# A gated mix of two attentions: VectorE's exps of attention B as a cubic, for scores bounded by a check

## The chip, the cores and the metric

The kernel runs on one core of one Trainium2 chip. The metric is the device time of one execution in microseconds (us). A "tile" below is one block of softmax numerators, 128 partitions by 1024 elements.

## The reference

Two attentions read the same input x (2048 tokens, 512 features) and are mixed by a gate per token:

```python
g = sigmoid((x * gate_w).sum(-1, keepdims=True))
a = A(x)   # 32 heads of 16 for q, one shared head for k and v; wq and wk are 8 times larger
b = B(x)   # 32 heads of 16 for q, k and v
out = g * a + (1 - g) * b
```

Each attention is softmax(q k^T / 4) v per head, followed by an output projection `wo`. All inputs are float32 draws of spread 0.05 (A's wq and wk then times 8). B's scores are therefore small, and A's are not.

## The kernel before

The scores of all heads are 2 x 32 x 2048 x 2048 numbers, which is 2048 tiles. No maximum is subtracted: an exp is taken of each score, the values are multiplied by it, and a column of ones beside the values gives the sum to divide by. That is safe only while scores are bounded, so the kernel collects absolute maxima of its inputs and intermediates in `stats` (`absmax`, L217), and near the end `flag_check` (L1058) turns them into a flag. When a bound is not met, `_general` runs after the fast path and computes all again.

**The work.** There are eight groups, alternating A and B, with eight heads each. A group has four phases (four of the heads, half of the queries), and a phase has 32 quads, which go over the keys. A quad is two tiles, with two heads each: their scores (a `score` call each, L630), their exps, and the products with the values (`values`, L682), summed over the phase in one PSUM pair of banks. At the end of a phase the sum is copied out (L747), normalised (`normalised`, reciprocals at L572), and the output products (`o_unit`, L496) add it into the output in DRAM. Products of the weights with x (`project`, L422) make q of both attentions and k and v of B for the phases to come; they are cut in steps of eight matmuls.

**Who takes the exps.** ScalarE takes nearly all (L641), from two PSUM tiles `sc` in turn. VectorE takes the rest: `vector_job` (L799) puts the scores of a tile into the spare PSUM pair `pair[1]`, and `chain` (L827) computes its exp in seven operations: a conversion from PSUM to a fixed-point power of two (L843), two integer passes that take out the mantissa and the exponent (L847, L851), and four multiply-adds (L856). Six tiles `vec` hold what VectorE works on. The spare pair is also where `project`, `o_unit` and the turning of v put their products, one at a time, until VectorE has emptied it.

**What sets the order.** The order of every instruction is fixed when the program is built, by a planner (`_Plan`, L80, and the loop of `pe_step`, L940) that keeps a clock for each engine and puts the next piece of work on TensorE or VectorE. ScalarE's scores come first. Between them TensorE takes, in this order, the values of VectorE's own quads, then the spare pair's work (`spare_job`, L900), then the values of ScalarE's quads. For the spare pair a tile of VectorE goes ahead of other products unless `hurry` (L891) finds one that would miss its due time. A tile of VectorE is begun only while

- at most 1500 ns of chain operations are queued on VectorE (`chained`, L796; 8500 for the second tile of a quad),
- at most three tiles are held by quads whose values aren't yet summed,
- the current phase has over 24,000 ns of ScalarE's exps left, beyond what is queued on VectorE; else a quad of the next phase is taken, if its q and k are there (`pick`, L768; in the last phase there is none).

On VectorE an operation has a rank (0 and 1: emptying a PSUM pair; 3: the chain; 3.2 to 3.5: normalising; 4: maxima), and the plan counts 1130 ns for a pass over a tile and 620 ns for an integer pass.

At the end the last group's output products are added to the output in SBUF (L515): `preload` (L1128) fetches it from DRAM once no other product is left, and the plan lets them begin 30 us later.

Of the kernel before, what the change touches and what calls it, by code (L numbers as in the profile page):

```python
# [20 lines left out]
P = 128  # L21
# [12 lines left out]
IN_MIN, IN_MAX = 2.0 ** -8, 16.0  # L34
QK_MAX = 4.0
S_MAX = 40.0


VEC = (0.14718679, 0.3602188, 0.76941108, -0.03925424)
LEAD = struct.unpack("I", struct.pack("f", 3.46474126))[0] & 0x7FFFFF  # L40
RANGED = ["v_a", "x", "gate", "wk_a", "wv_a", "wq_a", "wo_a", "wq_b", "wk_b", "wv_b", "wo_b", "v_b"]
KINDS = RANGED + ["q_a", "q_b", "k_a", "k_b"]
# [125 lines left out]
def _fast(ctx, tc, x, wq_a, wk_a, wv_a, wo_a, wqkv_b, wo_b, gate_w, out, flag):  # L168
# [33 lines left out]
    def rows(i):  # L202
        return slice(ROWS * i, ROWS * (i + 1))
# [218 lines left out]
    def project(part, src, gi, half, kind, can, due):  # L422

        state = {}
        need = ("w" + part, src, gi)
        name = f"{part}{src}{gi}{half}"

        def job(n):
            product(weights[src, gi, part], half, n, pair[1])

        def put(hilo, t):
            to = q_tiles(src, gi, half) if part == "q" else k_tiles(gi, half)
            parts = (0, 1, 0, 1) if part == "q" else (0, 0, 1, 1)
            for p in range(4):
                fns = lay(hilo, to[p], p, parts, (nc.sync, nc.gpsimd))
                done = max(plan.on_sp(fns[0::2], t, ISSUE_SP), plan.on_pool(fns[1::2], t, ISSUE))
                ready[part, src, gi, half, p] = done + LANDS
            free["hilo"] = done + LANDS - 4000

        def finish(t):  # L440
            hilo = []

            def hi():
                hilo.extend(halves_of(name))
                nc.vector.tensor_scalar(hilo[0], pair[1], UP ** -1, None, op0=ALU.mult)  # L445

            def lo():
                nc.vector.scalar_tensor_tensor(hilo[1], pair[1], UP ** -1, hilo[0], op0=ALU.mult, op1=ALU.subtract)

            def then(end):  # L450
                free["spare"] = end + FROM_VEC
                plan.vec(lambda: absmax(kind, 2 * gi + half, hilo[0], AX.XY), 1130, 4, end, due=end + 8000)
                if part == "v":
                    turned(gi, half, hilo, end)
                else:
                    put(hilo, end)

            free["hilo"] = math.inf
            one = plan.vec(hi, 1130, 1, t + TO_VEC)
            plan.vec(lo, 1130, 0, 0.0, (one,), then)  # L460

        return _Unit([(lambda n=n: job(n), PRODUCT) for n in range(len(STEPS))], finish,
                     lambda now: ready.get(need, math.inf) <= now and free["hilo"] <= now and can(), due, name, lambda now: can())

    def turned(gi, half, hilo, now):

# [293 lines left out]
        put_in[0] = 0  # L760


    def left_in(ph):

        lo = max(at[0], 32 * ph)
        return 2 * sum(1 for m in range(lo, 32 * ph + 32) if m not in vector) - (part[0] if lo == at[0] else 0)
# [60 lines left out]
    def chain(u, t):  # L827


        tiles = {}  # L830

        def tile(name):
            tiles[name] = free_vecs.popleft()
            return tiles[name]

        def give(*names):
            free_vecs.extend(tiles[name] for name in names)

        converts[0] += 1

        def convert():
            converts[0] -= 1
            nc.vector.tensor_scalar(tile("p").bitcast(I32), pair[1], SCALE / (UP * UP) / math.log(2) * 2.0 ** 23, None, op0=ALU.mult)  # L843

        def mantissa():
            tile("m"), tile("w")
            nc.vector.tensor_scalar(tiles["m"].bitcast(I32), tiles["p"].bitcast(I32), 0x7FFFFF, 125 << 23,  # L847
                                    op0=ALU.bitwise_and, op1=ALU.bitwise_or)

        def power():  # L850
            nc.vector.tensor_scalar(tiles["w"].bitcast(I32), tiles["p"].bitcast(I32), 0x7F800000, 0x40000000 | LEAD,  # L851
                                    op0=ALU.bitwise_and, op1=ALU.bitwise_xor)

        def horner(i):
            p, m, w = (tiles[k] for k in "pmw")
            nc.vector.scalar_tensor_tensor(p, m if i == 3 else p, VEC[i], m if i else w, op0=ALU.add, op1=ALU.mult)  # L856
            if i < 2:
                give("m" if i else "w")

        def spared(end):  # L860
            free["spare"] = end + FROM_VEC

        def over(end):
            probs[u] = tiles["p"]
            held[1] -= 1
            m = u // 2
            chains[m] = max(chains.get(m, 0), end)
            if all(x in probs for x in (2 * m, 2 * m + 1)):
                pending[quads[m][0]].append((m, end + FROM_VEC))

        def waits():
            return converts[0]

        def due(ns):
            return lambda: plan.act + left_in(quads[u // 2][0]) * EXP + (64 * EXP if quads[u // 2][0] > quads[min(at[0], len(quads) - 1)][0] else 0) - ns - 5000

        a = plan.vec(convert, 1130, 1, t + TO_VEC, (), spared, room=lambda: free_vecs)
        b = plan.vec(mantissa, 620, 3, 0.0, (a,), None, due(7000), lambda: len(free_vecs) >= 2 + waits())
        c = plan.vec(power, 620, 3, 0.0, (a, b), None, due(6300))
        d = plan.vec(lambda: horner(3), 1131, 3, 0.0, (b, c), None, due(5600))  # L880
        for i in (2, 1, 0):
            d = plan.vec(lambda i=i: horner(i), 1131, 3, 0.0, (d,), None if i else over, due(1300 * i + 1300))
# [175 lines left out]
    def flag_check():  # L1058
# [5 lines left out]
        nc.vector.tensor_scalar(lim[:, 2 * r : r + k], highest[:, r:k], QK_MAX, None, op0=ALU.is_lt)  # L1064
        nc.vector.tensor_mul(highest[:, ix("q_a") : ix("q_b") + 1], highest[:, ix("q_a") : ix("q_b") + 1],
                             highest[:, ix("k_a") : ix("k_b") + 1])
        nc.vector.tensor_scalar(lim[:, r + k : r + k + 2], highest[:, ix("q_a") : ix("q_b") + 1],
                                S_MAX / (DH * SCALE), None, op0=ALU.is_le)
        nc.vector.tensor_reduce(lim[:, 2 * k - 1 :], lim[:, 0 : r + k + 2], axis=AX.X, op=ALU.min)
        nc.vector.tensor_scalar(flag, lim[:, 2 * k - 1 :], -1.0, 1.0, op0=ALU.mult, op1=ALU.add)  # L1070

# [56 lines left out]
    def preload():  # L1128
        if "late" in ready or pv_at[0] < LASTS - 1 or current:
            return  # L1130
        if any(u for u in units) or any(op.rank == 1 for op in plan.ops) or wanted or loading:
            return
        for k in range(8):
            for e in range(2):
                t = 8 * (k // 4) + 4 * e + k % 4
                nc.sync.dma_start(late[:, k, e], out[t * P : (t + 1) * P, :])
        ready["late"] = plan.pe + 30000
# [65 lines left out]
    ready["ka", 0] = ready["va", 0] = 0.0  # L1203
    plan.vec(lambda: absmax("q_a", 0, hilo[0], AX.XY), 1130, 4, 8000.0, due=30000.0)
    plan.vec(k_top, 280, 4, 8000.0, due=30000.0)
    for k in range(5):
        plan.vec(lambda k=k: x_top(k), 1130, 4, 12000.0, due=50000.0)
    for k in range(4):
# [259 lines left out]
```

## Time and profile before

| | |
|---|---|
| runs, device time | 1824.4, 1826.82, 1826.92 us; median 1826.82 |
| span of the profiled execution, first to last instruction | 1822.2 us |
| granted TensorE clock, mean | 0.996 |
| TensorE matmuls | 1742.1 us busy (96%) |
| TensorE weight loads | 844.5 us busy (46%) |
| VectorE | 1332.0 us busy (73%) |
| ScalarE | 1778.7 us busy (98%) |
| exps on VectorE | 122 tiles |

The profile gives the profiled execution's span; its device time isn't given apart, and the three runs lie 2.2 to 4.7 us above that span. In the profile PE is TensorE, PEld its weight loads, DVE VectorE, ACT ScalarE, POOL GpSimd, and SP the queue of SyncE. A group of instructions has its source line, engine, operation, tiles and shape, its count, its busy time with the mean duration of one, and the idle time of its engine just before it with what ended that. Durations overlap: the next operation may start before the one ahead has ended. B's groups run from about 256 to 478, 701 to 919, 1141 to 1360 and 1583 us to the end.

### The profile page before, as it was taken

How to read it: one execution, taken by the hardware profiler on the slowest of the kernel's cores; microseconds unless marked ns; L12 is line 12 of the kernel's file. 1: busy time of each engine (PE TensorE's matmuls, PEld its weight loads, DVE VectorE, ACT ScalarE, POOL GpSimd, SP SyncE). 2: the span in 40 equal slices, each digit the busy share in tenths (PEclk: the TensorE clock that was granted, in tenths of full speed). 3: DMA queues.
4: the chain of work that ended last, by engine and by line, in shares of the span. 5: the costliest groups of instructions: out<-in, count | busy, mean ns of one | idle time of the engine just before them, and what ended most of it. 6: DMA issues, size and time to landing. Idle time of an engine off the chain costs nothing.

```text
span 1822.2 us, 95700 instructions
## 1 busy us (share of the span) xinstructions
PE 1742.1 (96%) x44697; PEld 844.5 (46%) x44697; DVE 1332.0 (73%) x1507; ACT 1778.7 (98%) x1942; POOL 305.1 (17%) x367
## 2 busy tenths in 40 slices
PE   8999999999999999999999999999999999999896
PEld 5544444444444444444444444444444444444442
DVE  5277656779667597869767569796967676788994
ACT  5999999999999999999999999999999999999995
POOL 2212001202020131231102023133200111012000
PEclk9999999999999999999999999999999999999998
DMA  5121111323121142433212123342312122236111
GB/s 152 36 61 44 46 58 55 90 55 67 32 62 32 39 83 55 75 65 66 44 42 63 32 66 56 67 84 63 64 20 57 44 55 57 42 67 149 36 61 61
DMA packets 64883, 109.39 MB, mean 60 GB/s; under 512 B 14480, under 2 KB 22928, under 8 KB 64480
## 3 DMA queue, kind: packets, MB, share of 16 engines
q0 software_dynamic: 21504, 43.99, 13.6%
q1 hardware_dynamic: 39744, 56.99, 11.4%
q8 instruction: 351, 5.75, 1.3%
q10 hardware_dynamic: 3232, 2.23, 0.4%
q14 instruction: 52, 0.43, 0.1%
HBM read 14.75 MB, written 33.55 MB: 27 GB/s over the span
## 4 chain that ended last, share of the span: by engine, by line
ACT 86%; issue 8%; PE 4%; DVE 1%; DMA 1%; ACTq 0%; POOL 0%; DVEq 0%
ACT prob L641 85%; PE pair L682 1%; PE sc L627 1%; PE pair L301 0%; DVE vec L856 0%; PE pair L1173 0%; DMA prob<-in_A_wv_dram 0%; DVE xT L1295 0%; DMA vec<-in_A_x_dram 0%; DVE xT L515 0%; DMA Qa<-loqa 0%; PE pair L335 0%; DVE dT L572 0%; ACT early L641 0%; PE pair L210 0%
## 5 line engine op out<-in xcount | busy, mean ns | idle before, releaser
L641 ACT ACTIVATE prob<-sc 128x1024 f32<-128x1024 f32 x1905 | 1749.7, 1134 | 3.8 <-PE sc L627 3.2
L682 PE MATMUL pair<-prob,vA 64*32 64x512 f32 (+1 forms) x8048 | 510.4, 566 | 0.0
L682 PE MATMUL pair<-prob,vB 64*32 64x512 f32 (+1 forms) x8016 | 508.4, 569 | 0.0
L856 DVE SCALAR_TENSOR_TENSOR vec<-vec,vec 128x1024 f32<-128x1024 f32 x366 | 445.9, 1242 | 2.8
L627 PE MATMUL sc<-Qb,K 64*32 64x512 f16 x7632 | 395.9, 380 | 37.2 <-ACT prob L641 26.8
L627 PE MATMUL sc<-Qa,kA 64*32 64x512 f16 x7776 | 401.8, 380 | 21.7 <-ACT prob L641 11.6
L627 PEld LDWEIGHTS <-K 64*32 64x32 f16 x8192 | 201.2, 89 | 414.8 <-issue 375.1
L627 PEld LDWEIGHTS <-kA 64*32 64x32 f16 x8192 | 199.8, 89 | 390.2 <-issue 346.6
L843 DVE TENSOR_SCALAR vec<-pair 128x1024 int32<-128x1024 f32 x122 | 148.4, 1216 | 64.5 <-PE pair L627 64.4
L682 PEld LDWEIGHTS pair<-prob,vA 64*32 64x32 f32 x8048 | 155.3, 105 | 20.0 <-issue 1.4
L682 PEld LDWEIGHTS pair<-prob,vB 64*32 64x32 f32 x8016 | 153.5, 105 | 19.0 <-DVE raw L747 0.7
L856 DVE SCALAR_TENSOR_TENSOR vec<-vec 128x1024 f32<-128x1024 f32 x122 | 151.8, 1247 | 0.6
L531 POOL DMA_DIRECT2D out_dram<-sum x48 | 60.6, 1284 | 387.6 <-DVE sum L521 373.0
L572 DVE RECIPROCAL dT<-dT 128x256 f32<-128x256 f32 (+1 forms) x66 | 111.4, 1694 | 18.9 <-DMA dT<-raw 18.6
L747 DVE COPY raw<-pair 128x1024 f32<-128x1024 f32 x31 | 37.9, 1224 | 95.8 <-PE pair L682 95.2
L847 DVE TENSOR_SCALAR vec<-vec 128x1024 int32<-128x1024 int32 x122 | 84.1, 692 | 2.8 <-PE pair L682 1.3
L851 DVE TENSOR_SCALAR vec<-vec 128x1024 int32<-128x1024 int32 x122 | 84.5, 695 | 0.0
L521 DVE TENSOR_SCALAR sum<-pair,gate_up 128x512 f32<-128x512 f32 x112 | 78.6, 740 | 6.3 <-PE pair L210 6.0
L404 POOL DMA_DIRECT2D Qa<-hiqa x31 | 17.3, 558 | 305.6 <-DVE hiqa L445 284.5
L210 PEld LDWEIGHTS <-o 64*32 64x32 f16 x3072 | 50.1, 93 | 39.3 <-ACT o L578 8.1
L404 POOL DMA_DIRECT2D Qb<-hiqb x32 | 18.4, 574 | 293.3 <-DVE o L578 169.1
L210 PE MATMUL pair<-w16ob,o 64*32 64x512 f16 x1488 | 61.1, 384 | 6.0 <-ACT o L578 6.0
(160 smaller groups left out, 1182.7 us busy)
## 6 DMA issues: line engine op xcount, KB each, us to landing
out_dram<-sum POOLq DMA_DIRECT2D x48, 512.0 KB, 5.8
vB<-vB SPq DMA_DIRECT2D x16, 384.0 KB, 4.9
dT<-raw SPq DMA_DIRECT2D x32, 128.0 KB, 3.1
oT<-raw SPq DMA_DIRECT2D x32, 128.0 KB, 3.4
out_dram<-sum SPq DMA_DIRECT2D x8, 512.0 KB, 2.9
xT<-out_dram SPq DMA_DIRECT2D x16, 256.0 KB, 3.3
dT<-raw SPq DMA_DIRECT2D x62, 64.0 KB, 2.2
out_dram<-xT SPq DMA_DIRECT2D x12, 256.0 KB, 2.4
```

The costliest lines, as they stand in the source:

```text
L210: nc.tensor.matmul(outs[n : n + COLS, i], lhs[i][rows(i), n : n + COLS], rhs[i][rows(i)], start=start, stop=stop)
L521: nc.vector.tensor_scalar(state["sum"][:, e], pair[1][:, e], g, None, op0=ALU.mult)
L531: done = plan.on_pool([lambda: nc.gpsimd.dma_start(dst, state["sum"], accum_op=ALU.add)], t, 1300)
L572: nc.vector.reciprocal(d[:, c : c + cut], d[:, c : c + cut])
L627: nc.tensor.matmul(bank[a : a + COLS, hh], k[rows(hh), key : key + COLS], Q[src, gi, half, p][rows(hh), j * BLK : (j + 1) * BLK], start=Tr ...
L641: nc.scalar.activation(probs[u], sc, AF.Exp, scale=SCALE / (UP * UP))
L682: nc.tensor.matmul(pair[0][32 * k : 32 * k + 32, i, cols], v[rows(i)], probs[2 * m + k // 2][rows(i), hh, cols], start=first, stop=last)
L747: nc.vector.tensor_copy(state["raw"], full)
L843: nc.vector.tensor_scalar(tile("p").bitcast(I32), pair[1], SCALE / (UP * UP) / math.log(2) * 2.0 ** 23, None, op0=ALU.mult)
L847: nc.vector.tensor_scalar(tiles["m"].bitcast(I32), tiles["p"].bitcast(I32), 0x7FFFFF, 125 << 23, op0=ALU.bitwise_and, op1=ALU.bitwise_or)
L851: nc.vector.tensor_scalar(tiles["w"].bitcast(I32), tiles["p"].bitcast(I32), 0x7F800000, 0x40000000 | LEAD, op0=ALU.bitwise_and, op1=ALU.bi ...
L856: nc.vector.scalar_tensor_tensor(p, m if i == 3 else p, VEC[i], m if i else w, op0=ALU.add, op1=ALU.mult)
```

## The change

For a quad of B the seven operations of `chain` become three: `p = a*s + c1` from PSUM, `w = (p + c2) * p`, `p = (w + c3) * p`, a cubic in the score s that has its root at p = 0. A keeps its seven. The cubic is for scores up to 0.16 in size. So the check of B's scores is made finer: for q of B, the maximum of single elements (`absmax`) is replaced by the maximum over tokens and heads of the sum of magnitudes over a head's 16 elements (`magnitudes`: a bitwise pass that clears the signs of the float16 pairs, four matmuls with a matrix of heads into the spare pair, and a reduction on VectorE), and `flag_check` asks that this, times the largest element of k, be at most 0.16 / SCALE. The matrix of heads is made at the start in a tile that is no longer used. `preload` no longer waits for the last group's own output products. The planner's rules are otherwise the same.

```diff
...
 IN_MIN, IN_MAX = 2.0 ** -8, 16.0
 QK_MAX = 4.0
 S_MAX = 40.0
+B_MAX = 0.16
 
 
 VEC = (0.14718679, 0.3602188, 0.76941108, -0.03925424)
+CUBE = (0.5500864384102879, 0.8808852829622843, -0.986763876, 1.22848465)
 LEAD = struct.unpack("I", struct.pack("f", 3.46474126))[0] & 0x7FFFFF
 RANGED = ["v_a", "x", "gate", "wk_a", "wv_a", "wq_a", "wo_a", "wq_b", "wk_b", "wv_b", "wo_b", "v_b"]
 KINDS = RANGED + ["q_a", "q_b", "k_a", "k_b"]
...
 
             def then(end):
                 free["spare"] = end + FROM_VEC
-                plan.vec(lambda: absmax(kind, 2 * gi + half, hilo[0], AX.XY), 1130, 4, end, due=end + 8000)
+                if kind == "q_b":
+                    plan.vec(lambda: magnitudes(2 * gi + half, hilo[0]), 330, 2, end, due=end + 4000, room=lambda: free_vecs)
+                else:
+                    plan.vec(lambda: absmax(kind, 2 * gi + half, hilo[0], AX.XY), 1130, 4, end, due=end + 8000)
                 if part == "v":
                     turned(gi, half, hilo, end)
                 else:
...
 
         return _Unit([(lambda n=n: job(n), PRODUCT) for n in range(len(STEPS))], finish,
                      lambda now: ready.get(need, math.inf) <= now and free["hilo"] <= now and can(), due, name, lambda now: can())
+
+    def magnitudes(n, hi):
+
+
+        tile = free_vecs.popleft()
+        mag = tile.rearrange("p a q -> p (a q)")[:, :BLK]
+        nc.vector.tensor_scalar(mag.bitcast(I32), hi.rearrange("p e t -> p (e t)").bitcast(I32), 0x7FFF7FFF, None, op0=ALU.bitwise_and)
+        mag = mag.bitcast(F16).rearrange("p (e t) -> p e t", e=2)
+
+        def job():
+            for i in range(2):
+                for e in range(2):
+                    nc.tensor.matmul(pair[1][COLS * e : COLS * (e + 1), i], heads16[rows(i)], mag[rows(i), e], start=True, stop=True)
+            free_vecs.append(tile)
+
+        def finish(t):
+            def top():
+                nc.vector.tensor_reduce(stats[: 2 * COLS, KINDS.index("q_b"), n : n + 1], pair[1][: 2 * COLS], axis=AX.XY, op=ALU.max)
+
+            def then(end):
+                free["spare"] = end + FROM_VEC
+
+            plan.vec(top, 1130, 1, t + TO_VEC, (), then)
+
+        start = plan.dve + 330 + FROM_VEC
+        units.append(_Unit([(job, PRODUCT)], finish, lambda now: now >= start, lambda: start + 12000, f"m{n}"))
 
     def turned(gi, half, hilo, now):
 
...
         pv_at[0] += 1
         put_in[0] = 0
 
+
+    def source(ph):
+        return groups[phases[ph][0]][0]
 
     def left_in(ph):
 
...
         def due(ns):
             return lambda: plan.act + left_in(quads[u // 2][0]) * EXP + (64 * EXP if quads[u // 2][0] > quads[min(at[0], len(quads) - 1)][0] else 0) - ns - 5000
 
+        if source(quads[u // 2][0]) == "b":
+
+            def first():
+                converts[0] -= 1
+                nc.vector.tensor_scalar(tile("p"), pair[1], CUBE[0] * SCALE / (UP * UP), CUBE[1], op0=ALU.mult, op1=ALU.add)
+
+            def second():
+                nc.vector.scalar_tensor_tensor(tile("w"), tiles["p"], CUBE[2], tiles["p"], op0=ALU.add, op1=ALU.mult)
+
+            def third():
+                p, w = tiles["p"], tiles["w"]
+                nc.vector.scalar_tensor_tensor(p, w, CUBE[3], p, op0=ALU.add, op1=ALU.mult)
+                give("w")
+
+            a = plan.vec(first, 1130, 1, t + TO_VEC, (), spared, room=lambda: free_vecs)
+            b = plan.vec(second, 1131, 3, 0.0, (a,), None, due(2600), lambda: len(free_vecs) >= 1 + waits())
+            plan.vec(third, 1131, 3, 0.0, (b,), over, due(1300))
+            return
         a = plan.vec(convert, 1130, 1, t + TO_VEC, (), spared, room=lambda: free_vecs)
         b = plan.vec(mantissa, 620, 3, 0.0, (a,), None, due(7000), lambda: len(free_vecs) >= 2 + waits())
         c = plan.vec(power, 620, 3, 0.0, (a, b), None, due(6300))
...
         nc.vector.tensor_scalar(lim[:, 2 * r : r + k], highest[:, r:k], QK_MAX, None, op0=ALU.is_lt)
         nc.vector.tensor_mul(highest[:, ix("q_a") : ix("q_b") + 1], highest[:, ix("q_a") : ix("q_b") + 1],
                              highest[:, ix("k_a") : ix("k_b") + 1])
-        nc.vector.tensor_scalar(lim[:, r + k : r + k + 2], highest[:, ix("q_a") : ix("q_b") + 1],
-                                S_MAX / (DH * SCALE), None, op0=ALU.is_le)
+        for src, most in (("q_a", S_MAX / (DH * SCALE)), ("q_b", B_MAX / SCALE)):
+            n = ix(src) - ix("q_a")
+            nc.vector.tensor_scalar(lim[:, r + k + n : r + k + n + 1], highest[:, ix(src) : ix(src) + 1], most, None, op0=ALU.is_le)
         nc.vector.tensor_reduce(lim[:, 2 * k - 1 :], lim[:, 0 : r + k + 2], axis=AX.X, op=ALU.min)
         nc.vector.tensor_scalar(flag, lim[:, 2 * k - 1 :], -1.0, 1.0, op0=ALU.mult, op1=ALU.add)
 
...
     def preload():
         if "late" in ready or pv_at[0] < LASTS - 1 or current:
             return
-        if any(u for u in units) or any(op.rank == 1 for op in plan.ops) or wanted or loading:
+        if any(not u.name.startswith(f"o{len(groups) - 1}") for u in units) or any(op.rank == 1 for op in plan.ops) or wanted or loading:
             return
         for k in range(8):
             for e in range(2):
...
     ready["ka", 0] = ready["va", 0] = 0.0
     plan.vec(lambda: absmax("q_a", 0, hilo[0], AX.XY), 1130, 4, 8000.0, due=30000.0)
     plan.vec(k_top, 280, 4, 8000.0, due=30000.0)
+
+    heads16 = level[:, P // 2 : P // 2 + COLS]
+
+    def heads_of():
+        each = level.bitcast(F32)[:, : P // DH]
+        nc.vector.tensor_reduce(each, ident.rearrange("p (h d) -> p h d", d=DH), axis=AX.X, op=ALU.max)
+        nc.vector.tensor_copy(heads16.rearrange("p (k h) -> p k h", h=P // DH), each.unsqueeze(1).to_broadcast([P, COLS * DH // P, P // DH]))
+
+    plan.vec(heads_of, 400, 4, 8000.0, due=30000.0)
     for k in range(5):
         plan.vec(lambda k=k: x_top(k), 1130, 4, 12000.0, due=50000.0)
     for k in range(4):
```

## The prediction, made before the result was known

> **What bounds the kernel now.** I read the page first: its sums, the chain that ended last, and the costliest groups.
>
> ```profile
> span 1822.2 us, 95700 instructions
> ...
> PE 1742.1 (96%) x44697; PEld 844.5 (46%) x44697; DVE 1332.0 (73%) x1507; ACT 1778.7 (98%) x1942; POOL 305.1 (17%) x367
> ...
> ACT 86%; issue 8%; PE 4%; DVE 1%; DMA 1%; ACTq 0%; POOL 0%; DVEq 0%
> ...
> L641 ACT ACTIVATE prob<-sc 128x1024 f32<-128x1024 f32 x1905 | 1749.7, 1134 | 3.8 <-PE sc L627 3.2
> ...
> L856 DVE SCALAR_TENSOR_TENSOR vec<-vec,vec 128x1024 f32<-128x1024 f32 x366 | 445.9, 1242 | 2.8
> ...
> L627 PE MATMUL sc<-Qb,K 64*32 64x512 f16 x7632 | 395.9, 380 | 37.2 <-ACT prob L641 26.8
> L627 PE MATMUL sc<-Qa,kA 64*32 64x512 f16 x7776 | 401.8, 380 | 21.7 <-ACT prob L641 11.6
> ...
> L843 DVE TENSOR_SCALAR vec<-pair 128x1024 int32<-128x1024 f32 x122 | 148.4, 1216 | 64.5 <-PE pair L627 64.4
> ...
> L856 DVE SCALAR_TENSOR_TENSOR vec<-vec 128x1024 f32<-128x1024 f32 x122 | 151.8, 1247 | 0.6
> ...
> L847 DVE TENSOR_SCALAR vec<-vec 128x1024 int32<-128x1024 int32 x122 | 84.1, 692 | 2.8 <-PE pair L682 1.3
> L851 DVE TENSOR_SCALAR vec<-vec 128x1024 int32<-128x1024 int32 x122 | 84.5, 695 | 0.0
> ```
>
> ScalarE is the bound: 98% busy, 86% of the chain that ended last, and its exps waited 3.8 us in all. One tile costs it 1749.7 / 1905 = 0.9185 us (the 1134 ns of one overlap). So the change is worth 0.9185 us for each tile that it moves from ScalarE to VectorE, and nothing otherwise. VectorE now does 122 of the 2048 tiles; it is 73% busy, so its own shorter time is worth nothing by itself. The question is how many more tiles the plan gives it, and who pays. I asked the lines view for the split of the 122, and the waits view for TensorE.
>
> ```profile
> L627 PE MATMUL pair<-Qb,K 64*32 64x512 f16 x560 | 29.3, 377 | 1.0 <-DVE vec L843 1.0
> L627 PE MATMUL pair<-Qa,kA 64*32 64x512 f16 x416 | 22.4, 376 | 0.0
> ```
>
> ```profile
> PE sc L627 <- ACT prob L641: 38.4, 108, 0.5
> ```
>
> Eight matmuls make a tile: 560 / 8 = 70 tiles are of B, 416 / 8 = 52 of A. TensorE waited for ScalarE 108 times, 38.4 us. Each such wait is a place where the plan had nothing to put. The timeline of TensorE shows what a place is; I took a stretch of B with every kind in it.
>
> ```profile
> 829.08 0.63 PE L210 MATMUL pair<-w16oa,o 64*32 64x512 f16 x16
> 829.63 0.41 PE L627 MATMUL sc<-Qb,K 64*32 64x512 f16 x8
> 829.84 1.05 PE L682 MATMUL pair<-prob,vB 64*32 64x512 f32 x16
> 830.70 0.41 PE L627 MATMUL sc<-Qb,K 64*32 64x512 f16 x8
> 831.46 0.41 PE L627 MATMUL sc<-Qb,K 64*32 64x512 f16 x8 [0.35 <-ACT prob L641]
> ...
> 836.20 0.41 PE L627 MATMUL sc<-Qb,K 64*32 64x512 f16 x8
> 836.96 0.41 PE L627 MATMUL sc<-Qb,K 64*32 64x512 f16 x8 [0.35 <-ACT prob L641]
> ...
> 838.24 0.64 PE L682 MATMUL pair<-vec,vB 64*32 64x256 f32 x16
> ...
> 840.08 0.64 PE L682 MATMUL pair<-vec,vB 64*32 64x256 f32 x16
> ...
> 841.91 0.41 PE L627 MATMUL pair<-Qb,K 64*32 64x512 f16 x8
> ...
> 843.74 0.41 PE L627 MATMUL pair<-Qb,K 64*32 64x512 f16 x8
> ```
>
> ScalarE's pair of tiles sets a beat: 829.63 to 831.46 is 1.83 us. In a beat TensorE does a score (829.63), the values of an older pair (829.84), the second score (830.70), and then has one slot of some 0.55 us before the next beat (829.08 to 829.63). All other work goes through these slots, in pieces of two 0.215 us steps: projections, output products, and both parts of VectorE's own tiles. A quad (two tiles) given to VectorE takes four slots: two scores (841.91, 843.74) and two halves of its values (838.24, 840.08). It also removes its own beat, so it costs five slots in all. The scarce thing is slots, not VectorE.
>
> **Which empty slots the change can fill.** Dividing by 38.4 / 108 = 0.356 us a wait, the idle time before scores puts 26.8 / 0.356 = 75 empty slots into B and 11.6 / 0.356 = 33 into A. I sorted them in the timeline. Most (81) start right behind the last step of a product: the one spare PSUM pair is then being emptied by VectorE, as at 831.46, behind the output product of 829.08. The other 27, all in B, start a beat or more later (at 836.96, say): the pair is free, no product is ready, and the next VectorE tile may not start, since the plan holds it back while over 1500 ns of VectorE chain is queued. First and last of the 27:
>
> ```profile
> 258.39 0.41 PE L627 MATMUL sc<-Qb,K 64*32 64x512 f16 x8 [0.35 <-ACT prob L641]
> ...
> 1780.72 0.41 PE L627 MATMUL sc<-Qb,K 64*32 64x512 f16 x8 [0.35 <-ACT prob L641]
> ```
>
> That VectorE's chain is what holds, its own timeline says:
>
> ```profile
> 820.48 1.22 DVE L843 TENSOR_SCALAR vec<-pair 128x1024 int32<-128x1024 f32 x1
> ...
> 823.27 1.16 DVE L843 TENSOR_SCALAR vec<-pair 128x1024 int32<-128x1024 f32 x1
> ...
> 836.34 1.23 DVE L856 SCALAR_TENSOR_TENSOR vec<-vec,vec 128x1024 f32<-128x1024 f32 x1
> ```
>
> Two tiles converted at 820.5 and 823.3 end at 837.6: 17 us for a pair of B.
>
> **The change, part by part.**
>
> *The chain.* Removed per B tile: the two integer passes (692 + 695 ns) and two of four Horner steps (2 x 1242 ns); the conversion (1216 ns) becomes a scale and add of the same shape from PSUM, for which I keep 1216. A tile goes from 1216 + 692 + 695 + 4 x 1242 = 7571 ns to 1216 + 2 x 1242 = 3700 ns. For 70 tiles that frees 271 us of VectorE, which hides under ScalarE and gives no time directly. By the plan's figures what is queued behind a conversion falls from 5764 to 2262 ns, so the next quad may start about four slots after the last one; in the rows above it is 820.5 to 841.9, twelve beats.
>
> *What that fills.* Of the 27 blocked slots six stay (the rows of 1771 to 1781 lie in the last 24 us before which the plan closes a phase, a constant that isn't changed): 21. Of the 75 - 27 = 48 slots of B lost to emptying the spare pair, some close because a free VectorE empties it at once, and because values of VectorE tiles need no spare pair and can fall there. This can be between none and about half (24); I take a quarter, 12, since an output product has two passes to empty and just misses the next slot even on an idle VectorE.
>
> *Bounding the scores.* Eight times, for each half of q_b, the reduction of one row below is replaced by a bitwise pass on 512 words, four matmuls and a reduction from PSUM.
>
> ```profile
> L219 DVE TENSOR_REDUCE stats<-hiqb 128x1 f32<-128x1024 f16 x8 | 9.7, 1215 | 0.0
> ```
>
> VectorE: the pass between zero and 692 ns (the 1024-word pass), I take 346; the reduction 1215. That is 0.35 us more each, 2.8 us in all, hidden (with a full VectorE it would be 2.8 us). TensorE: each takes a slot and the spare pair: 8 slots lost. It also holds one of six VectorE tiles until its matmuls are done; while quads wait on a fifth tile that could hold up one conversion, which I count as nothing. The two small operations that make the matrix of heads run at the start, and one more tiny comparison in the final check; each lies beside ScalarE's exps. The looser condition for fetching the partial output moves nothing unless output products are late (a rival below).
>
> *Sum.* 21 + 12 - 8 = 25 slots, 25 / 5 = 5 quads, 10 tiles, 10 x 0.9185 = 9.2 us. Against the profiled execution: 1822.2 - 9.2 = 1813.0 us of span. The median of the runs, 1826.82, lies 4.6 us above that span, so I forecast 1826.8 - 9.2 = 1817.6 us. Ends of this case: (21 - 8) / 5 = 2.6 quads, 4.8 us; (21 + 24) / 5 = 9 quads, 16.5 us.
>
> *A rule to weigh.* TensorE's page row says 96% busy as matmuls and 46% as weight loads. The Trainium skill (Perfetto Trace Analysis, Identifying the Most-Contended Engine) says matmul busy time is a bad measure of TensorE's headroom, and weight-load share a good one; by that TensorE would be half free and the sum would go by VectorE alone. This trace speaks against it: the slots, not either share, are what run out, with 108 empty ones left. Its rule on consistent bubbles (same page, Optimization Strategy: a gap that repeats can mean too little PSUM) agrees with the 81 slots lost behind the spare pair.
>
> **The rivals.**
>
> *VectorE is the limit, TensorE is not.* The 271 us would then make 271 / 3.70 = 73 more tiles, 67 us, 1760 us. That is the weight-load rule above taken at its word. Against it: 73 tiles are 36 quads and 182 slots, and there are 108. With every empty slot filled it is 108 / 5 = 21.6 quads, 43 tiles, 39.7 us: 1787 us. For it: the plan puts its quads before products that aren't urgent, and values can fall into slots where the pair is being emptied. I give 0.12 to anything beyond 16.5 us.
>
> *No net gain.* B's quads now come first and push products into A's groups; A's chain is as long as before, and its quads give way. What B wins A loses, and the 8 slots are paid. Tiles stay at 122 give or take three: 1827 us. For it: A has only 33 empty slots. Against: nothing in A was blocked by the chain, so idle slots truly exist only in B. 0.20.
>
> *Slower: the last outputs come late.* In the last group no projection is due and output products have due times beyond the end, so quads are put ahead of them. The partial output is fetched only when the products of the older groups are done, and 30 us of the plan later the last group's own may start.
>
> ```profile
> 1695.08 1.23 DVE L747 COPY raw<-pair 128x1024 f32<-128x1024 f32 x1 [0.18 <-PE pair L682]
> ...
> 1732.58 1.41 DVE L515 SCALAR_TENSOR_TENSOR xT<-pair,gate_up,xT 128x512 f32<-128x512 f32 x2
> ...
> 1758.57 1.41 DVE L515 SCALAR_TENSOR_TENSOR xT<-pair,gate_up,xT 128x512 f32<-128x512 f32 x2
> ...
> 1788.00 1.41 DVE L515 SCALAR_TENSOR_TENSOR xT<-pair,gate_up,xT 128x512 f32<-128x512 f32 x2 [6.66 <-PE pair L210]
> ...
> 1800.83 1.41 DVE L515 SCALAR_TENSOR_TENSOR xT<-pair,gate_up,xT 128x512 f32<-128x512 f32 x2 [2.26 <-PE pair L210]
> ```
>
> Now four of these eight come by 1758.6 and four from 1788.0 to 1800.8, which is 12.8 / 3 = 4.3 us apart. If the older products slip by over 1788 - 1758 = 30 us, 16 beats, the first four go behind the others, past ScalarE's end: 4 x 4.3 = 17 us, less the 9.2 won, 1835 us; with one or two of them late it is between 1822 and 1826. Four more quads ahead of them would be enough. Against: 16 beats is more than the slots that I expect to go to quads there. 0.17.
>
> *The change doesn't do what it says.* Were the bound on B's scores not met, the general path would follow the fast one and the time would be a multiple. With inputs of spread 0.05 q and k have a spread of 0.05 x 0.05 x sqrt(512) = 0.057; sixteen magnitudes sum to about 1.4 at most, the largest k is near 0.28, and 1.4 x 0.28 x 0.25 = 0.10 is under 0.16. 0.01.
>
> **How the numbers follow.** My forecast has 0.50, 1817.6 us, its own range 1810 to 1822. A difference of 0.2% (3.7 us) is about what a measurement of this kernel can tell. The range goes on to 1796 (half way into the filled-slots case) and to 1832 (most of the late outputs); outside lie some 0.05 below and 0.1 above. Faster by over 0.2%: 0.50 + 0.12 = 0.62. Same: 0.19, nearly all of the no-gain case. Slower: 0.19, the late outputs, the failed bound and a loss of a few tiles.
>
> **What would show it.** Exps on ScalarE should fall from 1905 to about 1895, with 0.918 us each; conversions of B should go from 70 to 80 or a little over, A's stay near 52; VectorE's busy share should fall below 65%; TensorE's waits for ScalarE should fall from 108 to 80 or 90. The new chain should show three passes of about 1.2 us. I am wrong if A's tiles drop as B's rise, if waits of ScalarE for scores grow beyond a few us, or if L515's first four end after 1790.

## The result and the profile after

The changed kernel takes 1830.84 us (median of 20 runs) against 1824.88 us before (20 runs): ratio 1.0031, 95% interval 1.0024 to 1.0037. It is slower by 6 us, where 9.2 us less had been forecast. (The median before is now of 20 runs; the 1826.82 us ahead of the prediction was of the first three.) The profiled execution has a span of 1830.1 us, 7.9 us more than that of before; that is more than the 6 us of the medians, since this execution, at 1831.97 us, was one of the longer ones.

From the page of the changed kernel, then its lines view and its waits view:

```profile
span 1830.1 us, 95801 instructions
...
PE 1747.5 (95%) x44873; PEld 851.7 (47%) x44873; DVE 1111.8 (61%) x1252; ACT 1769.2 (97%) x1932; POOL 294.6 (16%) x367
...
ACT 84%; issue 8%; PE 5%; DVE 2%; DMA 0%; SPq 0%; ACTq 0%; DVEq 0%
...
L672 ACT ACTIVATE prob<-sc 128x1024 f32<-128x1024 f32 x1895 | 1740.3, 1134 | 8.5 <-PE sc L658 8.0
...
L915 DVE TENSOR_SCALAR vec<-pair 128x1024 f32<-128x1024 f32 x84 | 102.3, 1218 | 58.0 <-PE pair L658 58.0
...
L918 DVE SCALAR_TENSOR_TENSOR vec<-vec 128x1024 f32<-128x1024 f32 x84 | 103.3, 1233 | 1.0
L922 DVE SCALAR_TENSOR_TENSOR vec<-vec,vec 128x1024 f32<-128x1024 f32 x84 | 101.9, 1216 | 0.8
```

```profile
L658 PE MATMUL pair<-Qb,K 64*32 64x512 f16 x672 | 35.0, 376 | 0.3 <-DVE vec L915 0.3
L658 PE MATMUL pair<-Qa,kA 64*32 64x512 f16 x384 | 19.8, 376 | 0.0
```

```profile
DVE dT L603 <- DMA dT<-raw: 66.6, 17, 6.9
...
PE sc L658 <- ACT prob L672: 33.7, 91, 1.4
...
ACT prob L672 <- PE sc L658: 8.0, 8, 1.8
```

The same two waits of VectorE and ScalarE in the waits view of before:

```profile
DVE dT L572 <- DMA dT<-raw: 18.6, 6, 4.4
...
ACT prob L641 <- PE sc L627: 3.2, 8, 1.2
```

The chain is as forecast: three passes, 1218 + 1233 + 1216 = 3667 ns (3700 was worked out). VectorE does 672 / 8 = 84 tiles of B and 384 / 8 = 48 of A, 132 in all, and ScalarE's exps fall from 1905 to 1895: the ten tiles of the forecast, though not where it had them: B has 14 more than its 70, and A 4 fewer than its 52. (These rows count the exps written to `prob`. In both kernels 21 more write other tiles, so ScalarE takes 2048 - 122 = 1926 exps in all before and 2048 - 132 = 1916 now. The exps of the runs below are counted in this second way.) VectorE's busy share is 61%. And yet the kernel is slower. Where the time went is in the last part of the timeline, first of VectorE, then of ScalarE, then of TensorE:

```profile
1787.87 1.41 DVE L546 SCALAR_TENSOR_TENSOR xT<-pair,gate_up,xT 128x512 f32<-128x512 f32 x2 [14.56 <-PE pair L212]
1795.34 1.41 DVE L546 SCALAR_TENSOR_TENSOR xT<-pair,gate_up,xT 128x512 f32<-128x512 f32 x2 [6.06 <-PE pair L212]
...
1812.77 1.41 DVE L546 SCALAR_TENSOR_TENSOR xT<-pair,gate_up,xT 128x512 f32<-128x512 f32 x2 [1.60 <-PE pair L212]
```

```profile
1789.73 5.61 ACT L672 ACTIVATE prob<-sc 128x1024 f32<-128x1024 f32 x6 [0.24 <-issue]
```

```profile
1808.21 1.48 PE L212 MATMUL pair<-w16ob,o 64*32 64x512 f16 x24 [1.53 <-DVE xT L546]
1811.22 1.48 PE L212 MATMUL pair<-w16ob,o 64*32 64x512 f16 x24 [1.53 <-DVE xT L546]
```

The last exps of before, in its timeline of ScalarE:

```profile
1779.52 21.31 ACT L641 ACTIVATE prob<-sc 128x1024 f32<-128x1024 f32 x23
```

The last exp ends at 1789.73 + 5.61 = 1795.3 us, 5.5 us earlier than before's 1779.52 + 21.31 = 1800.8. But the first of the last group's eight output products is taken at 1787.9 and not at 1732.6, and seven of the eight come at 1795.3 or later. There is one spare PSUM pair for them, so each waits for VectorE to empty it (the 1.53 us), 2.4 to 3.0 us apart. The tail behind the last exp, 1822.2 - 1800.8 = 21.4 us before, is 1830.1 - 1795.3 = 34.8 us: 13.4 us more, less 5.5, is the 7.9 us of span. Below, "tail" is this stretch from the end of the last exp to the end of the span.

### The profile page after: what moved, and what is told of

It reads as the page before. It is cut to its first block, busy times and chain, and to the rows that moved or that the text cites. A ratio compares the mean times of both kernels' runs of the same rounds, so it can differ in the third digit from the quotient of the medians.

```text
span 1830.1 us, 95801 instructions
## 1 busy us (share of the span) xinstructions
PE 1747.5 (95%) x44873; PEld 851.7 (47%) x44873; DVE 1111.8 (61%) x1252; ACT 1769.2 (97%) x1932; POOL 294.6 (16%) x367
## 4 chain that ended last, share of the span: by engine, by line
ACT 84%; issue 8%; PE 5%; DVE 2%; DMA 0%; SPq 0%; ACTq 0%; DVEq 0%
ACT prob L672 84%; PE pair L713 2%; PE sc L658 1%; PE pair L212 1%; DVE vec L890 0%; PE pair L303 0%; DVE xT L546 0%; PE pair L1226 0%; DVE xT L1357 0%; PE pair L337 0%; PE pt L303 0%; DMA Qa<-loqa 0%; DVE dT L603 0%; ACT early L672 0%; DVE vec L877 0%
## 5 line engine op out<-in xcount | busy, mean ns | idle before, releaser
L713 PE MATMUL pair<-prob,vB 64*32 64x512 f32 (+1 forms) x7904 | 502.6, 568 | 1.7 <-issue 1.7
L658 PE MATMUL sc<-Qa,kA 64*32 64x512 f16 x7808 | 402.9, 380 | 23.0 <-ACT prob L672 13.4
L658 PE MATMUL sc<-Qb,K 64*32 64x512 f16 x7520 | 390.7, 380 | 32.4 <-ACT prob L672 20.3
L890 DVE SCALAR_TENSOR_TENSOR vec<-vec,vec 128x1024 f32<-128x1024 f32 x144 | 177.0, 1251 | 0.8
L603 DVE RECIPROCAL dT<-dT 128x256 f32<-128x256 f32 (+1 forms) x66 | 110.0, 1685 | 66.7 <-DMA dT<-raw 66.6
L915 DVE TENSOR_SCALAR vec<-pair 128x1024 f32<-128x1024 f32 x84 | 102.3, 1218 | 58.0 <-PE pair L658 58.0
L918 DVE SCALAR_TENSOR_TENSOR vec<-vec 128x1024 f32<-128x1024 f32 x84 | 103.3, 1233 | 1.0
L922 DVE SCALAR_TENSOR_TENSOR vec<-vec,vec 128x1024 f32<-128x1024 f32 x84 | 101.9, 1216 | 0.8
L877 DVE TENSOR_SCALAR vec<-pair 128x1024 int32<-128x1024 f32 x48 | 58.2, 1213 | 19.4 <-PE pair L658 19.2
L447 DVE TENSOR_SCALAR hivb<-pair 128x1024 f16<-128x1024 f32 x8 | 9.8, 1225 | 91.4 <-PE pair L212 91.4
```

The source lines that it names most:

```text
L603: nc.vector.reciprocal(d[:, c : c + cut], d[:, c : c + cut])
L658: nc.tensor.matmul(bank[a : a + COLS, hh], k[rows(hh), key : key + COLS], Q[src, gi, half, p][rows(hh), j * BLK : (j + 1) * BLK], start=Tr ...
L713: nc.tensor.matmul(pair[0][32 * k : 32 * k + 32, i, cols], v[rows(i)], probs[2 * m + k // 2][rows(i), hh, cols], start=first, stop=last)
L915: nc.vector.tensor_scalar(tile("p"), pair[1], CUBE[0] * SCALE / (UP * UP), CUBE[1], op0=ALU.mult, op1=ALU.add)
L918: nc.vector.scalar_tensor_tensor(tile("w"), tiles["p"], CUBE[2], tiles["p"], op0=ALU.add, op1=ALU.mult)
L922: nc.vector.scalar_tensor_tensor(p, w, CUBE[3], p, op0=ALU.add, op1=ALU.mult)
```

## The experiments

All ratios are to the kernel before, timed beside each run on the same chip (three chips were used). The profile shows that the end is late; open was what makes it late. Theory 1: the finer check displaces output products into the last group. Theory 2, the mechanism of the prediction's slower rival: VectorE's quads, put ahead, displace them.

**The two halves of the change, one at a time.** First the cubic without the finer check: q of B is measured by its largest element, as before, and the matrix of heads isn't made (not shown). This run leaves out the guarantee that B's scores lie within the cubic's 0.16.

```diff
-                if kind == "q_b":
-                    plan.vec(lambda: magnitudes(2 * gi + half, hilo[0]), 330, 2, end, due=end + 4000, room=lambda: free_vecs)
-                else:
-                    plan.vec(lambda: absmax(kind, 2 * gi + half, hilo[0], AX.XY), 1130, 4, end, due=end + 8000)
+                plan.vec(lambda: absmax(kind, 2 * gi + half, hilo[0], AX.XY), 1130, 4, end, due=end + 8000)
...
-        for src, most in (("q_a", S_MAX / (DH * SCALE)), ("q_b", B_MAX / SCALE)):
+        for src, most in (("q_a", S_MAX / (DH * SCALE)), ("q_b", S_MAX / (DH * SCALE))):
...
```

> The cubic stays; the finer check is left out (q of B is measured by its largest element, as before, and B's bound is the old one). Theory 1, the finer check displaces products: its eight products through the spare pair and the waits around them push output products into the last group; without them the last group's outputs begin at about 1735 us, the tail behind the last exp is 21.4 us as before, 1912 exps on ScalarE end near 1792 us, and the time is about 9 us under before (ratio 0.995). Theory 2, the quads displace them: VectorE's tiles put ahead are enough; the last outputs still begin after 1780 us, the tail stays near 35 us, and the time is no better than before (ratio 1.000 to 1.003).

Ratio 0.9955 (0.9942 to 0.9968), 1815.92 us. 1912 exps, the last ends at 1791.8 us, the tail is 22.2 us, and the last outputs begin on time. From its timeline of VectorE and its waits view:

```profile
1732.71 1.41 DVE L543 SCALAR_TENSOR_TENSOR xT<-pair,gate_up,xT 128x512 f32<-128x512 f32 x2 [3.45 <-PE pair L212]
```

```profile
DVE dT L600 <- DMA dT<-raw: 45.9, 15, 5.1
PE sc L655 <- ACT prob L669: 27.8, 76, 0.5
ACT prob L669 <- PE sc L655: 8.0, 12, 1.2
```

That is theory 1's case. The last group has 20 tiles on VectorE here as in the changed kernel, so these quads put ahead are not enough to make it late. The looser condition of `preload` is in this run too, so it isn't the cause either.

Then the finer check with the old chain (`if False:` in place of the test for B):

> The finer check stays; the chain of B is the old one with seven operations. Theory 1: the check alone pushes products into the last group, so that the last outputs begin later than the 1733 us of before, and it costs slots: 1928 exps, 2 more than before, 1.8 us, and a tail of 21 to 24 us; ratio 1.001 to 1.003. Theory 2: the check has next to no price; the last outputs begin near 1733 us, and the ratio is 1.000 to 1.001.

Ratio 1.0037 (1.0024 to 1.0050), 1831.92 us: the check alone costs some 7 us, more than was expected even of theory 1. The tail stays at 21.4 us, though the last outputs begin at 1760.6 us, 28 us later than before. The cost lies ahead of it: 1928 exps, and ScalarE waited 8.2 us for scores (3.2 before).

**What of the check costs.** To the run without the finer check I gave back only a place in the spare pair: eight bare products with the check's due time, and the reductions that empty the pair, with no bitwise pass and no VectorE tile held.

```diff
+                if kind == "q_b":
+                    slot(2 * gi + half, hilo[0])
...
+    def slot(n, hi):
+        def job():
+            for i in range(2):
+                for e in range(2):
+                    nc.tensor.matmul(pair[1][COLS * e : COLS * (e + 1), i], ident16[rows(i), :COLS], hi[rows(i), e], start=True, stop=True)
...
+                nc.vector.tensor_reduce(sparestat[: 2 * COLS], pair[1][: 2 * COLS], axis=AX.XY, op=ALU.max)
...
```

> The run without the finer check, plus eight bare products of the check's size through the spare pair, one per half of q of B, each with its reduction; no bitwise pass and no VectorE tile held. Their result goes nowhere, and B's bound is the old one. If a place in the spare pair is the whole price of the check, this loses all that the run without it had won: 1920 exps instead of 1912, output products displaced into the last group again, a tail near 29 us instead of 22, ratio to before 1.001 to 1.004. If the price is the bitwise pass or the held tile, the ratio stays at 0.995 to 0.997.

Ratio 1.0034 (1.0021 to 1.0048): 1920 exps, tail 30.0 us, all as theory 1 had it. The lines view of its last group, next to that of the changed kernel, then before:

```profile
L212 PE MATMUL pair<-w16ob,o 64*32 64x512 f16 x480 | 21.0, 433 | 9.3 <-DVE xT L563 6.3 <-ACT o L626 3.1
L212 PE MATMUL pair<-w16oa,o 64*32 64x512 f16 x384 | 15.5, 376 | 0.0
L212 PE MATMUL pair<-xT,w16qb 64*32 64x512 f16 x32 | 1.3, 376 | 0.0
```

```profile
L212 PE MATMUL pair<-w16ob,o 64*32 64x512 f16 x528 | 22.3, 433 | 11.0 <-DVE xT L546 8.0 <-ACT o L609 3.0
L212 PE MATMUL pair<-w16oa,o 64*32 64x512 f16 x384 | 15.4, 376 | 0.0
L212 PE MATMUL pair<-xT,w16qb 64*32 64x512 f16 x192 | 7.6, 376 | 0.0
```

```profile
L210 PE MATMUL pair<-w16oa,o 64*32 64x512 f16 x384 | 15.3, 376 | 0.0
L210 PE MATMUL pair<-w16ob,o 64*32 64x512 f16 x336 | 14.7, 412 | 6.0 <-ACT o L578 6.0
L210 PE MATMUL pair<-xT,w16qb 64*32 64x512 f16 x112 | 4.2, 376 | 0.0
```

In steps of eight matmuls the last group has (384 + 336 + 112) / 8 = 104 before and (528 + 384 + 192) / 8 = 138 in the changed kernel: 34 steps, 17 slots of two steps, that earlier groups had pushed in front of the last outputs. Without the finer check it is 104 again; with the bare products it is (480 + 384 + 32) / 8 = 112, with 18 steps of output products more than before and 10 steps of q fewer. Products and reduction weren't parted here: what is shown is the price of both, one place in the spare pair.

Then the other way about, the changed kernel with the check's products due at once (`lambda: 0` for `lambda: start + 12000`), so that their VectorE tile comes back sooner:

> The changed kernel, with the check's eight products due at once, so that each goes ahead of VectorE's tiles and gives its tile back sooner than after the 5 to 10 us that it takes now. If the held tile is the check's price, the two tiles lost in the first group come back and the time falls to that without the finer check (ratio 0.996). If the price is the slots and the products displaced into the last group, the exps fall a little (1914) but the last outputs still begin after 1780 us and the tail stays near 35 us: ratio 1.001 to 1.003.

Ratio 1.0043 (1.0028 to 1.0057), tail 35.0 us, last outputs from 1786.9 us; the two tiles lost in the first group did come back. The held tile isn't the price: without one, the bare products lose those two tiles of the first group as well.

**The late end.** Four runs on where it comes from. Output products of older groups due by phase 29:

```diff
-        due = 32 * (4 * n + 2 * half + 8)
+        due = 32 * min(4 * n + 2 * half + 8, LASTS - 2 if n + 1 < len(groups) else math.inf)
```

> The changed kernel, but the output products of the older groups get a due time at phase 29 at the latest, so that they go ahead of VectorE's tiles there. If the late fetch is the cause, the last outputs begin before 1760 us and the tail falls from 34.8 to about 21.5 us. But products that go first take slots from quads: 1924 exps instead of 1916, 7.3 us. Expected span 1795 + 7 + 21.5 = 1824 us, ratio to before 1.000 to 1.001. If the tail has another cause (the changed condition for the fetch, the check at the end), it stays near 35 us and the ratio is 1.007.

Ratio 1.0001 (0.9992 to 1.0010): last outputs from 1745.7 us, tail 22.0 us, 1924 exps. As expected, within a microsecond of span: the late end is cured, and the price is eight exps more than in the changed kernel.

The plan's 30 us between fetch and products made 12 (`plan.pe + 12000`):

> The changed kernel with the same quads in the same places; only the plan lets the last group's products begin 12 us after the partial output is fetched, not 30. If what costs is that these products stand behind the last exp, about two more of the eight come before it, some 3 us each: the tail falls from 34.8 to about 29 us and the ratio to before from 1.003 to 1.000. If the fetch itself takes as long as the 30 us, TensorE or VectorE waits for it and the time stays at ratio 1.003 or more.

Ratio 1.0015 (1.0006 to 1.0025), tail 30.2 us. About half of what was hoped for in the ratio, the tail as expected.

The old chain for B in the last group alone:

> The changed kernel with the old chain of seven operations in the last group alone. If the products that earlier groups pushed into the last one are the cause of the late end, the tail stays well above before's 21.4 us: about 29 us, 1920 exps end near 1799 us, ratio 1.002 to 1.003. If the quads put ahead in the last group itself are the cause, the last outputs begin before 1760 us, the tail is 21 to 23 us and the ratio 0.998 to 0.999.

Ratio 1.0029 (1.0019 to 1.0040), tail 28.5 us, last outputs from 1772.0 us. As expected of products that were displaced before the last group: with 16 tiles on VectorE there, not 20, the end is still late. But the tail is 6 us shorter than in the changed kernel, so the quads of the last group have a share in it.

The run with the check alone shows the other side of this. Its last group, in the lines view:

```profile
L212 PE MATMUL pair<-w16ob,o 64*32 64x512 f16 x480 | 19.9, 401 | 6.1 <-ACT o L609 6.1
L212 PE MATMUL pair<-w16oa,o 64*32 64x512 f16 x384 | 15.7, 376 | 0.0
L658 PE MATMUL pair<-Qb,K 64*32 64x512 f16 x128 | 7.1, 377 | 0.9 <-issue 0.9
L212 PE MATMUL pair<-xT,w16qb 64*32 64x512 f16 x112 | 4.2, 376 | 0.0
```

It has (480 + 384 + 112) / 8 = 122 steps, 18 more than before, and no longer tail; its VectorE takes 16 tiles there, where the run with the bare products has as many displaced output products, 24 tiles and a tail of 30.0 us. Counted in slots, two for a tile by the prediction's working, the last group's load is the sum of both:

| run | products + tiles, slots | first of the last outputs, us | tail, us |
|---|---|---|---|
| before | 52 + 36 = 88 | 1732.6 | 21.4 |
| without the finer check | 52 + 40 = 92 | 1732.7 | 22.2 |
| check with the old chain | 61 + 32 = 93 | 1760.6 | 21.4 |
| old chain in the last group | 69 + 32 = 101 | 1772.0 | 28.5 |
| bare products | 56 + 48 = 104 | 1778.0 | 30.0 |
| check's products due at once | 56 + 52 = 108 | 1786.9 | 35.0 |
| changed kernel | 69 + 40 = 109 | 1787.9 | 34.8 |

So the two theories aren't rivals: the first of the last outputs comes the later the larger the sum, and the tail grows in the rows with over 100. This is a count over seven runs, not a run made to test it; the two runs that change when output products may go are left out.

The fetches of the changed kernel through GpSimd's queue (`nc.gpsimd` for `nc.sync` in `preload`):

> The changed kernel with the same move of the fetches to GpSimd's queue. Its fetch comes at 1752 us, behind the rows of phase 30; the late end there is due to where the last products stand, not to the queue: tail still near 35 us, ratio 1.002 to 1.004. If the queue delayed them, the tail falls below 30 us and the ratio to 1.000.

Ratio 1.0028 (1.0018 to 1.0039), tail 34.9 us: the queue isn't what makes the end of the changed kernel late.

**A check without the eight products.** The maxima of q of B are kept per 128 tokens, in the reduction that was there before, and summed over a head once, near the end. This bounds the same scores a little less tightly.

```diff
+    def by_chunks(n, hi):
+        nc.vector.tensor_reduce(chunks[:, 8 * n : 8 * n + 8], hi.rearrange("p e (c t) -> p (e c) t", t=P), axis=AX.X, op=ALU.max,
+                                apply_absolute_value=True)
...
+        nc.vector.tensor_tensor(level[:, : P // 2].rearrange("p (g c) -> p g c", g=NG), chunks.rearrange("p (g c) -> p g c", g=NG),
+                                lim[:, :NG].unsqueeze(2).to_broadcast([P, NG, 16]), op=ALU.mult)
...
+            nc.tensor.matmul(pair[1][:COLS, 0, : P // 2], heads16, level[:, : P // 2], start=True, stop=True)
```

> The cubic with a finer check that needs no product per half of q: the reduction of q of B keeps maxima of 128 tokens each, and near the end one small product sums over a head's 16 elements these times the largest k of the same element. If the eight products through the spare pair are the check's price, this has what the run without the finer check has: 1912 exps, last outputs from about 1735 us, tail 22 us, ratio to before 0.995 to 0.996. If a finer check costs by its VectorE passes or its work at the end, the ratio lies between 0.997 and 1.004.

Ratio 0.9994 (0.9985 to 1.0003). A miss: 1912 exps and a tail of 22.6 us, but the last exp ended at 1798.9 and not 1792 us. The timeline around 1700 us says why, in the queue of SyncE, on VectorE and on TensorE:

```profile
1696.61 0.81 SPq L1191 DMA_DIRECT2D xT<-out_dram  x2
1697.82 3.01 SPq L598 DMA_DIRECT2D dT<-raw  x4
```

```profile
1702.36 1.75 DVE L605 RECIPROCAL dT<-dT 128x256 f32<-128x256 f32 x1 [13.43 <-DMA dT<-raw]
1704.03 1.16 DVE L917 TENSOR_SCALAR vec<-pair 128x1024 f32<-128x1024 f32 x1
```

```profile
1705.24 0.63 PE L660 MATMUL pair<-Qb,K 64*32 64x512 f16 x8 [4.70 <-DVE vec L917]
1705.63 0.67 PE L660 MATMUL sc<-Qb,K 64*32 64x512 f16 x8
```

The fetches of the partial output (L1191) wait for the last sums to land in DRAM (SyncE's own waits between 1680 and 1715 us have 25.4 us, in two, for `out_dram<-sum`); in SyncE's queue a phase's rows for the normalising (L598) stand behind them. VectorE has reached the reciprocal that needs those rows and waits 13.43 us; behind it in order stands the conversion that would empty the spare pair (L917); TensorE waits 4.70 us for that pair with a tile of VectorE, and ScalarE's scores stand behind. That VectorE reached the reciprocal this early because it is emptier is a reading, not shown apart. Moving the fetches to GpSimd's queue changes nothing else:

> The same as end_check in the order of every compute engine; only the 16 fetches of the partial output go through GpSimd's queue, not SyncE's. There they stood ahead of a phase's rows for the normalising, and waited for the last sums to land in DRAM; VectorE waited 13.4 us for those rows and ScalarE 4.7 us behind it. If that queue is why end_check missed its 0.995, the wait falls to 5 us or less, the last exp ends near 1792 us instead of 1799, ratio 0.995 to 0.996. If not, 0.999 again.

Ratio 0.9964 (0.9950 to 0.9977), last exp at 1792.8 us. ScalarE's waits for scores fell from 14.5 to 8.1 us. VectorE's wait in that place fell to 7.60 us, not to 5.

Giving the normalising more time in the plan, together with the 12 us, not 30, between fetch and products (`plan.pe + 12000`, not shown):

```diff
-            a = plan.vec(lambda c=c: over(c), 1560, 3.5, now + 7700, (), None, due)
-            b = plan.vec(lambda c=c: times(c), 330, 3.4, now + 12000, (a,), None, due)
+            a = plan.vec(lambda c=c: over(c), 1560, 3.5, now + 9000, (), None, due)
+            b = plan.vec(lambda c=c: times(c), 330, 3.4, now + 13000, (a,), None, due)
...
```

> As end_check, and the plan counts 1.3 us more before a reciprocal of the normalising and 1 us more before the multiplication behind it, and 12 us, not 30, for the fetch of the partial output; 1910 exps. Theory 3: on an emptier VectorE the normalising is issued before its rows have landed, and what stands behind it in order (emptying the spare pair, conversions) waits; VectorE's waits for these rows, 51 us in 17 places without the finer check and 19 us in 6 before, fall to under 30 us, ScalarE's waits for scores from 8 to about 5 us, ratio to before 0.993. If those waits cost ScalarE nothing, its waits stay at 8 us and the ratio is 0.9945 to 0.995, by the two exps alone.

Ratio 0.9956 (0.9942 to 0.9971). VectorE's waits for the rows fell to 13.7 us in 8 places, further than expected; ScalarE's waits for scores were 8.7 us, not 5. So theory 3 is right about VectorE. That the shorter waits were worth more than the two exps and the long wait that is gone isn't shown, and the run doesn't part them from the earlier products. The later normalising, the 12 us and the move to GpSimd's queue together:

> end_check_norm with the same move of the fetches to GpSimd's queue. There VectorE had no long wait for rows, so the move should change little: ratio 0.995 to 0.996, at best 0.5 us better.

```profile
span 1811.4 us, 95744 instructions
...
L674 ACT ACTIVATE prob<-sc 128x1024 f32<-128x1024 f32 x1889 | 1735.7, 1131 | 7.3 <-PE sc L660 6.4
```

Ratio 0.9936 (0.9922 to 0.9949), 1813.16 us: the best version, 12.6 us under the kernel before and, by the two ratios, some 17 us under the changed one. Its interval overlaps that of the run ahead of it, which leaves the queue's own share here open.

## Why the prediction was wrong

- **The bound and the price of a tile:** right. ScalarE's exps set the pace, ten moved to VectorE, and the last one ends 5.5 us sooner. Ten times 0.9185 is 9.2 us; ScalarE's waits for scores took back 8.0 - 3.2 = 4.8 us, which the sum had not counted. That would leave 4.4 us; the 1.1 us by which the last exp ends sooner still are not attributed.
- **Slots, not VectorE, limit the tiles:** right about VectorE. Its busy share fell to 61% and only ten tiles moved, so the rival by which VectorE alone would decide (73 more tiles) did not come. That slots are the limit isn't shown: of TensorE's 108 waits for ScalarE, its empty slots, 91 are left (80 or 90 were forecast).
- **The chain alone:** 21 + 12 slots would have been 33 / 5 = 6.6 quads, 13 tiles, 12 us. Measured without the finer check: 14 tiles and 8 us of span; ScalarE's waits, 8.0 us there too, account for the rest.
- **The step that failed: "TensorE: each takes a slot and the spare pair: 8 slots lost."** Eight slots were to cost 1.6 quads, 2.9 us, and the sum left the tail as it was. In the changed kernel the check cost 4 exps (1916 against 1912) and 34.8 - 22.2 = 12.6 us of tail. Eight bare products with their reductions cost 1.0034 / 0.9955, 0.8% or some 14 us, more than the 8 us that the chain had won: 8 exps, and 8 us of tail. The places of a plan aren't a heap from which eight are taken: other products moved later, and 17 slots' worth of them arrived in the last group of the changed kernel. Why one place displaces that many isn't shown. That the near due time holds quads back was only argued; making it zero was no better, and a later one wasn't tried.
- **The slower rival** had the right place and a chance of 0.17. Its point of decision, 30 us of slip, held: the slip was 1787.9 - 1732.6 = 55 us, and of the other runs the one with 28 us kept its tail and the one with 39 us did not. Its cause was the smaller part: one more quad stands in the last group (20 tiles, not 18), not four, and the same 20 tiles without the check did no harm; the other 17 of the 21 slots are products displaced earlier. It took it that no projection is due there, but 112 matmuls of q of B run in the last group even before. Its price came near by luck: it has four outputs, 4.3 us apart, behind ScalarE's end (17 us); measured are seven at or behind it, 2.4 to 3.0 us apart, the last 17.4 us behind it, and what follows that one is 4.0 us shorter than before, which makes the 13.4 us.
- **The signs of being wrong** that the prediction named all came: A's tiles fell by 4, ScalarE's waits for scores grew to 8.0 us, and three of the first four outputs came after 1790 us.
- **What was missing:** a rival in which a lighter engine runs into its own DMA waits. Before, VectorE waited 18.6 us in 6 places for rows; in the changed kernel 66.6 us in 17. One such wait, of 13.43 us, is shown to cost (0.9994 became 0.9964 when the fetches ahead of the rows were moved). What the others cost in the changed kernel isn't shown, and they don't explain ScalarE's 8.0 us: with the check alone VectorE waited 10.9 us for rows, less than before, and ScalarE 8.2 us for scores. The cause of those stays open.

## What to carry to other kernels

When an order is planned to the last slot, price an added job by what it pushes back and where that ends up, not by its own duration; the end of the program has no later slot to give. Look for work of that kind which can ride on an instruction that is there anyway, as the check's maxima could. And when an engine gets lighter, look at what it will now reach too early: as at 1702 us above, everything that stands behind it in order then waits too.

## What the runs showed of the hardware

After the 4.70 us without a matmul in the run with the check at the end, TensorE came back at half its clock. From its windows view (the columns behind POOL are the granted clock, DMA share and GB/s):

```profile
1700.00:1704.00 4.00, 0.55 (x16) 0.19 (x8) 1.64 (x1) 1.76 (x2) 0.00 (x0) 1.00 0.31 72
1705.00:1711.00 6.00, 5.76 (x80) 2.34 (x87) 6.00 (x6) 3.08 (x3) 0.00 (x0) 0.50 0.04 8
```

A set of eight scores took 0.67 us there (1705.63) and not 0.41, and ScalarE waited 6.8 us for scores between 1690 and 1712 us, 2 us more than the 4.7 us of the stall. The Trainium skill (TensorE: Matmul & The Clock Gate, Part 1) gives about 3.4 us of idleness as the window after which the clock is halved; this one case agrees.
